# Small empty products ahead of the first scores of a fused attention and two-stage expert kernel

## The chip, the cores and the metric

The kernel runs on one core of a Trainium2 chip. The metric is the time of one execution on the device in microseconds; of three runs of the kernel before, the median is 618.53 us (618.53 to 618.88). A profiled execution gives the trace: what each engine did and when, counted from the first instruction.

## The reference

```python
# attention: 2 batches, 8 heads, 576 positions, head size 64
scores = scale * np.matmul(q, k.transpose(0, 1, 3, 2))
# heads 0-3: the last 32 positions; heads 4-7: every 32nd position before
mask_local = (rel >= 0) & (rel < stride)
mask_strided = (rel >= 0) & (pos[None, :] % stride == pos[:, None] % stride)
attn = softmax(where(mask, scores, -1e9)); x = attn @ v          # -> (1152, 512)
# gated block
h = (x @ w1) * (x @ w2) @ w3;  x = h @ w_out
# four experts, weighted by the normalised domain probabilities
out += p[:, e:e + 1] * (np.maximum(x @ w1[e], 0.0) @ w2[e])
```

All inputs and outputs are float32; the weights of the gated block are 64-bit floats that the kernel turns into pairs of 32-bit parts itself.

## The kernel before, in words

The order of the instructions on every engine is written out by hand, in the order of the Python statements; a wait is inserted wherever one engine needs another's result. Each engine works through its own list in order.

The attention of a batch is cut into six chunks (`Chunk4`): chunks 0 to 2 are local heads, 3 to 5 strided ones. For a chunk, `scores` (L380) puts a mask product (L386 or L395) and then many small products of 64 rows (L391, L402) into one PSUM bank; `maxima`, `subtract`, `exps` and `sums` turn them into weights on VectorE and ScalarE, `normalise` (L450) runs on GpSimd for the first batch; `transposes` (L455), `evac` (L460), `pv` (local values L475, strided values L484) and `put` (L513) follow. The chunks are interleaved by hand: scores of chunks 0, 1, 2, 3, then the transposes of chunk 0, scores of 4, transposes of 1, scores of 5, values of 0 and so on.

Queries and keys of the first local heads are loaded in two halves, cut at position 288 (`load_qk(0, 0, CUT)`): chunk 0 needs the first half, chunk 1 the second. Value loads and the first weight load follow on SyncE's queue; the weight load waits behind a one-element write on GpSimd (`hold`, L128), which stands in GpSimd's list behind the normalisation of chunk 2.

An empty product multiplies a zeroed tile `idle` by itself into a bank that nobody reads. `warm_up` issues two of 512 columns right after the tile is zeroed, ahead of the first scores (`keep_warm(WARM)`, L120); `keep_warm` puts in three more between the chunks' scores and the transposes, one of 512 and two of 256 columns. A product of float32 operands is recorded as two matmuls, each with a weight load of its own.

After the attention of the first batch, the products of x with the first two weights (`whole_product`, L616), the gated block (`ab_block`, L305 to L307), the third weight, and the experts follow, on TensorE nearly without a gap.

Of the kernel before, what the change touches and what calls it, by code (L numbers as in the profile page):

```python
# [19 lines left out]
W = 32  # L20
# [10 lines left out]
NBLK = NT // BLK  # L31
NTT = NT // P
NEG = -8.0e9
WARM = 2
SCALE = 1.0 / float(D) ** 0.5

EXP_LO, EXP_HI = 3.0517578125e-05, 122880.0
# [7 lines left out]
def kernel(  # L45
# [14 lines left out]
    mm = nc.tensor.matmul  # L60
# [13 lines left out]
    def bank(name):  # L74
        return ps.tile([P, 512], F32, tag="ps", name=name)
# [33 lines left out]
    def warm_up():  # L109

        idle = tmp.tile([P, P], F32, tag="pT", name="idle")
        nc.vector.memset(idle, 0.0)
        nc.scalar.activation(small.tile([P, 1], F32, tag="rec", name="one"), idle[:, :1], AF.Exp)
        moving = idle.unsqueeze(1).to_broadcast([P, 4, P])

        def keep_warm(n, parts=4):
            if n:
                acc = bank("idle").rearrange("p (a b) -> p a b", a=4)[:, :parts]
            for i in range(n):
                mm(acc, idle, moving[:, :parts], start=i == 0, stop=i == n - 1)  # L120

        keep_warm(WARM)
        return keep_warm


# [725 lines left out]

    with tc.manual_schedule():
        keep_warm = warm_up()
        load_qk(0, 0, CUT)
        local_masks()
# [166 lines left out]
        for n in range(2):  # L1022
            acc = bank("ab_acc")[:, :HB]
# [37 lines left out]
        for it in range(8):  # L1061
# [8 lines left out]
            i = {1: 0, 3: 1, 6: 2}.get(it)  # L1070
# [139 lines left out]
```

## Time and profile before

| | |
|---|---|
| median of 3 runs | 618.53 us (618.53 to 618.88) |
| profiled execution | 618.26 us, of which the span of its instructions 616.1 us |
| TensorE matmuls | busy 609.8 us (99%), 4488 recorded |
| VectorE | busy 443.1 us (72%) |
| ScalarE | busy 280.6 us (46%) |
| GpSimd | busy 9.9 us (2%) |
| share of the chain that ended last | TensorE 90%, VectorE 4%, ScalarE 3%, DMA 2%, issue 1% |

The chain is followed back from the last instruction, at each step to what released it. "issue" is time in which an engine waited for nothing that the profile shows. Overlapping matmuls are drawn with their full length each, so a group's time in the timeline runs a little past the start of the next group.

### The profile page before, as it was taken

The page shows a single profiled execution, that of the slowest core. Times are in us where ns is not written, and L with a number is a line of the kernel's source. Part 1 is how long each engine was busy: PE and PEld are TensorE (multiplying, and loading weights), DVE is VectorE, ACT ScalarE, POOL GpSimd, SP SyncE. Part 2 cuts the span into 40 slices and gives each one's busy share as a digit, 9 for nine tenths or more (in the row PEclk, how much of TensorE's full clock was granted, in tenths as well). Part 3 has the DMA queues.
Part 4 walks back from the last instruction along what each step waited for, and adds up shares of the span by engine and source line. Part 5 has one row for each costly group of instructions (what it writes and reads, how often), then busy time and mean ns, then how long its engine had stood idle before and what let it go on. Part 6 is the DMA issues. An engine that isn't in the chain of part 4 may idle for free.

```text
span 616.1 us, 11131 instructions
## 1 busy us (share of the span) xinstructions
PE 609.8 (99%) x4488; PEld 555.9 (90%) x4488; DVE 443.1 (72%) x811; ACT 280.6 (46%) x568; POOL 9.9 (2%) x33
## 2 busy tenths in 40 slices
PE   8999999999999999999999999999999999999997
PEld 5799999998889999998899988999889898989997
DVE  4899987998863237777877987887766665755843
ACT  3879966665733134333433333434343333333320
POOL 4100000000000000000000000000000000000000
PEclk9999999999999999999999999999999999999999
DMA  9896330334522202333545334435585557464411
GB/s 272 321 325 185 139 138 2 111 132 172 202 68 102 86 19 69 137 138 136 199 153 194 128 149 172 167 142 212 178 318 202 213 192 248 162 234 176 156 51 68
DMA packets 28510, 99.63 MB, mean 162 GB/s; under 512 B 2660, under 2 KB 6316, under 8 KB 26028
## 3 DMA queue, kind: packets, MB, share of 16 engines
q1 hardware_dynamic: 27916, 98.34, 44.5%
q8 instruction: 35, 0.57, 0.4%
q10 hardware_dynamic: 544, 0.59, 0.3%
q14 instruction: 15, 0.12, 0.1%
HBM read 79.78 MB, written 19.14 MB: 161 GB/s over the span
## 4 chain that ended last, share of the span: by engine, by line
PE 90%; DVE 4%; ACT 3%; DMA 2%; issue 1%; DVEq 0%; ACTq 0%; SPq 0%
PE g_acc L305 11%; PE g_acc L306 11%; PE g_acc L307 11%; PE m_a L307 4%; PE m_a L306 4%; PE m_a L305 4%; PE ab_acc L305 3%; PE ab_acc L307 3%; PE ab_acc L306 3%; PE m_b L306 3%; PE m_c L305 3%; PE m_c L306 3%; PE m_b L305 3%; PE x_acc L305 3%; PE m_c L307 3%; PE m_b L307 3%
## 5 line engine op out<-in xcount | busy, mean ns | idle before, releaser
L761 ACT ACTIVATE h_hi<-u 128x320 fp32r<-128x320 f32 (+1 forms) x128 | 56.9, 445 | 188.9 <-DVE u L767 188.9
L305 PE MATMUL g_acc<-w_hi,h_hi 128*128 128x512 f32 (+1 forms) x296 | 114.3, 386 | 0.0
L306 PE MATMUL g_acc<-w_lo,h_hi 128*128 128x512 f32 (+1 forms) x296 | 114.2, 386 | 0.0
L307 PE MATMUL g_acc<-w_hi,h_lo 128*128 128x512 f32 (+1 forms) x296 | 113.7, 384 | 0.0
L700 DVE TENSOR_TENSOR w_lo<-raw,w_hi 128x768 fp32r<-128x768 f32 x64 | 69.3, 1084 | 12.3 <-ACT w_hi L698 12.3
L767 DVE TENSOR_TENSOR u<-m_b,u 128x320 f32<-128x320 f32 (+1 forms) x96 | 40.7, 451 | 50.4 <-PE m_b L307 50.4
L305 PE MATMUL ab_acc<-x_hi,w_hi 128*128 128x288 f32 x240 | 71.6, 298 | 0.4 <-ACT ab L601 0.2
L307 PE MATMUL ab_acc<-x_hi,w_lo 128*128 128x288 f32 x240 | 70.7, 295 | 0.0
L306 PE MATMUL ab_acc<-x_lo,w_hi 128*128 128x288 f32 x240 | 70.7, 294 | 0.0
L307 PEld LDWEIGHTS g_acc<-w_hi,h_lo 128*128 128x128 f32 x296 | 55.6, 188 | 11.6
L305 PEld LDWEIGHTS g_acc<-w_hi,h_hi 128*128 128x128 f32 x296 | 55.8, 188 | 8.0
L306 PEld LDWEIGHTS g_acc<-w_lo,h_hi 128*128 128x128 f32 x296 | 55.7, 188 | 7.6
L763 DVE SCALAR_TENSOR_TENSOR h_lo<-u,h_hi 128x320 fp32r<-128x320 f32 (+1 forms) x128 | 57.6, 450 | 3.6 <-ACT h_hi L761 1.1
L698 ACT CAST w_hi<-raw 128x768 fp32r<-128x768 f32 x64 | 59.9, 936 | 0.0
L305 PEld LDWEIGHTS ab_acc<-x_hi,w_hi 128*128 128x128 f32 x240 | 45.0, 188 | 1.0 <-ACT ab L601 0.5
L306 PEld LDWEIGHTS ab_acc<-x_lo,w_hi 128*128 128x128 f32 x240 | 45.0, 188 | 0.0
L307 PEld LDWEIGHTS ab_acc<-x_hi,w_lo 128*128 128x128 f32 x240 | 45.0, 188 | 0.0
L306 PE MATMUL m_b<-b_t,s_hi 128*128 128x320 f32 (+1 forms) x128 | 37.9, 296 | 0.0
L767 DVE TENSOR_TENSOR u<-m_a,u 128x320 f32<-128x320 f32 (+1 forms) x64 | 28.8, 449 | 11.6 <-PE m_a L307 11.6
L700 DVE TENSOR_TENSOR s_lo<-raw,s_hi 128x1024 fp32r<-128x1024 f32 x16 | 19.6, 1225 | 24.3 <-ACT s_hi L698 24.3
L767 DVE TENSOR_TENSOR u<-m_c,u 128x320 f32<-128x320 f32 (+1 forms) x64 | 28.9, 452 | 4.5 <-PE m_c L307 3.9
L777 ACT COPY u<-m_a 128x320 f32<-128x320 f32 (+1 forms) x32 | 12.7, 398 | 42.4 <-PE m_a L307 42.4
(180 smaller groups left out, 1384.6 us busy)
## 6 DMA issues: line engine op xcount, KB each, us to landing
raw<-in_e_dram SPq DMA_DIRECT2D x32, 1024.0 KB, 4.9
raw<-in_w3T_dram SPq DMA_DIRECT2D x8, 1024.0 KB, 4.9
stored<-s_hi SPq DMA_DIRECT2D x16, 512.0 KB, 2.6
stored<-s_lo SPq DMA_DIRECT2D x16, 512.0 KB, 2.6
s_hi<-stored SPq DMA_DIRECT2D x16, 512.0 KB, 3.7
s_lo<-stored SPq DMA_DIRECT2D x16, 512.0 KB, 4.9
raw<-in_w_dram SPq DMA_DIRECT2D x7, 1024.0 KB, 7.2
raw<-in_w_out_dram SPq DMA_DIRECT2D x4, 1024.0 KB, 5.0
```

Source lines behind the costliest of these rows:

```text
L305: mm(acc, lh, rh, start=first, stop=False)
L306: mm(acc, lh, rl, start=False, stop=False)
L307: mm(acc, ll, rh, start=False, stop=last)
L698: nc.scalar.copy(dst[0], src)
L700: nc.vector.tensor_tensor(out=dst[1], in0=src, in1=dst[0].bitcast(F32), op=ALU.subtract)
L761: nc.scalar.activation(hi, src, AF.Relu)
L763: nc.vector.scalar_tensor_tensor(out=lo, in0=src, scalar=0.0, in1=hi.bitcast(F32), op0=ALU.max, op1=ALU.subtract)
L767: nc.vector.tensor_tensor(out=out, in0=acc, in1=b, op=ALU.add)
L777: nc.scalar.copy(u1, a)
```

## The change

The two empty products of 512 columns ahead of the first scores become 18 of 32 columns, in turn on the lower and the upper 64 rows and columns of the array, and one of 256 columns. The later empty products stay.

```diff
-WARM = 2
+FILL = 18
...
-        keep_warm(WARM)
+        acc = bank("idle")
+        for i in range(FILL):
+            r = slice(64 * (i % 2), 64 * (i % 2) + 64)
+            mm(acc[r, :W], idle[r, :64], idle[r, :W], start=True, stop=True)
+        keep_warm(1, 2)
         return keep_warm
```

`W` is 32; `keep_warm(1, 2)` is one product of 2 x 128 columns. The lines of the kernel move down by four.

TensorE's list begins like this before, up to the scores of chunk 1 (`sc` is a chunk's scores, `tqk` the queries and keys, `i_loc` and `m_loc` the local mask):

```order
L1206 UNCONDITIONAL_BRANCH
L120 MATMUL idle<-idle 128x512 x2
L386 LDWEIGHTS i_loc
L386 MATMUL sc<-m_loc,i_loc 128x384
L391 MATMUL sc<-tqk 32x64 x24
L386 LDWEIGHTS i_loc
L386 MATMUL sc<-m_loc,i_loc 128x384
L391 MATMUL sc<-tqk 32x64 x24
```

And like this after the change, the same stretch:

```order
L1210 UNCONDITIONAL_BRANCH
L125 MATMUL idle<-idle 64x32 x18
L120 MATMUL idle<-idle 128x256
L390 LDWEIGHTS i_loc
L390 MATMUL sc<-m_loc,i_loc 128x384
L395 MATMUL sc<-tqk 32x64 x24
L390 LDWEIGHTS i_loc
L390 MATMUL sc<-m_loc,i_loc 128x384
L395 MATMUL sc<-tqk 32x64 x24
```

Nineteen products stand where two stood; what follows is the same. Further down, TensorE's list after the change has the scores of chunk 3, the transposes of chunk 0 (`tp`) and the scores of chunk 4 (`i_str` and `m_str` are the strided mask):

```order
L399 LDWEIGHTS i_str
L399 MATMUL sc<-m_str,i_str 128x432
L406 MATMUL sc<-tqk 54x54 x16
L459 MATMUL tp<-ident,p_ring 128x128 x3
L399 LDWEIGHTS i_str
L399 MATMUL sc<-m_str,i_str 128x432
L406 MATMUL sc<-tqk 54x54 x16
L459 MATMUL tp<-ident,p_ring 128x128 x3
```

These rows are those of before, with 17 more products ahead of them. The lists of the other engines are unchanged.

## Rows read from the trace of the kernel before

**Rows 1.** The page: span, busy time of the matmul engine, instruction queue (packets, MB).
```profile
span 616.1 us, 11131 instructions
...
PE 609.8 (99%) x4488; PEld 555.9 (90%) x4488; DVE 443.1 (72%) x811; ACT 280.6 (46%) x568; POOL 9.9 (2%) x33
...
q8 instruction: 35, 0.57, 0.4%
```
**Rows 2.** Groups of matmuls, 0 to 10.7 us (xcount | busy us, mean ns | idle before).
```profile
L120 PE MATMUL idle<-idle 128*128 128x512 f32 (+1 forms) x8 | 5.6, 819 | 1.0 <-DVE idle L112 1.0
L391 PE MATMUL sc<-tqk 64*32 64x64 f32 x144 | 3.3, 249 | 0.1
L386 PE MATMUL sc<-m_loc,i_loc 128*128 128x384 bf16 x3 | 1.3, 431 | 0.0
```
**Rows 3.** Timeline of the matmuls (start us, us, instruction, xcount, idle before).
```profile
1.05 3.78 PE L120 MATMUL idle<-idle 128*128 128x512 f32 x4 [1.05 <-DVE idle L112]
...
5.08 1.51 PE L391 MATMUL sc<-tqk 64*32 64x64 f32 x48
...
7.09 0.87 PE L391 MATMUL sc<-tqk 64*32 64x64 f32 x48
...
10.46 0.35 PE L395 MATMUL sc<-m_str,i_str 128*128 128x432 bf16 x1
10.73 1.01 PE L402 MATMUL sc<-tqk 64*54 64x54 f32 x32
11.67 0.55 PE L455 MATMUL tp<-ident,p_ring 128*128 128x128 f32 x3
12.05 0.35 PE L395 MATMUL sc<-m_str,i_str 128*128 128x432 bf16 x1
12.33 0.95 PE L402 MATMUL sc<-tqk 64*54 64x54 f32 x29
14.18 0.30 PE L402 MATMUL sc<-tqk 64*54 64x54 f32 x3 [0.90 <-issue]
```
**Rows 4.** Groups of matmuls between the two stops, 14.1 to 18.1 us.
```profile
L475 PE MATMUL o<-pT,tv_loc 64*64 64x32 f32 x85 | 1.7, 220 | 0.0
L402 PE MATMUL sc<-tqk 64*54 64x54 f32 (+1 forms) x35 | 1.2, 198 | 0.9 <-issue 0.9
L455 PE MATMUL tp<-ident,p_ring 128*128 128x128 f32 x6 | 1.1, 291 | 0.0
L395 PE MATMUL sc<-m_str,i_str 128*128 128x432 bf16 x1 | 0.3, 346 | 0.0
```
**Rows 5.** The chain of waits up to 24 us (start us, us, what).
```profile
1.54 5.41 DMA tqk<-in_qT_dram
...
10.80 0.94 PE sc L402 x32
...
17.84 0.30 issue
...
20.66 0.60 PE tp L455 x4
...
23.03 0.81 PE o L484 x32
```
**Rows 6.** Instruction packets in 11.36:12.74, 15.3:16.75, 19.4:20.45 us (share of 16 engines).
```profile
q8 instruction: 1, 0.02, 6.2%
...
q8 instruction: 1, 0.02, 5.6%
...
q8 instruction: 1, 0.02, 5.5%
```
**Rows 7.** Timeline of VectorE: the maxima of chunks 3 and 4.
```profile
11.79 0.61 DVE L408 TENSOR_REDUCE mx<-sc 128x8 f32<-128x432 f32 x1 [0.21 <-PE sc L402]
...
14.52 0.61 DVE L408 TENSOR_REDUCE mx<-sc 128x8 f32<-128x432 f32 x1 [0.60 <-PE sc L402]
```
**Rows 8.** Busy time of each engine from 23.9 to 600 us.
```profile
23.90:600.00 576.10, 575.52 (x3895) 529.75 (x3896) 422.09 (x766) 266.43 (x527) 0.00 (x0) 1.00 0.44 160
```

## The prediction

> **What bounds the kernel now.** I read the page first, then the matmul engine's timeline, the chain of waits, and last the instruction packets among the DMA traffic. The page says that TensorE is busy for 609.8 of 616.1 us [rows 1]. From 23.9 us to 600 us it idles for 0.6 us in all [rows 8]. So whatever shifts the start of that dense stretch shifts the end by the same amount, and a change in the first 23 us is worth what it does to the chain there: the strided value products that start at 23.03 us [rows 5], behind which the dense work queues.
>
> Before that, three things hold TensorE up. Until 6.96 us the chain is the load of the second half of the queries [rows 5]; the second chunk's scores start at 7.09 us [rows 3] and nothing ahead of them in the program can bring that forward. Then TensorE runs without a gap to 13.28 us, stops for 0.90 us inside the fifth chunk's scores, 29 of 32 records done [rows 3], and stops again for 0.30 us at 17.84 us [rows 5]. Both stops have the releaser "issue": no engine and no load that the profile shows is waited for.
>
> What those two stops have in common is an instruction count. The trace records 4488 matmuls and 4488 weight loads, and the instruction queue q8 fetched 35 packets of 0.57 MB / 35 = 16 KB [rows 1]; 8976 / 35 = 256 records to a packet. Between the two stops lie 85 + 35 + 6 + 1 = 127 matmuls [rows 4], with their loads 254 records, plus a few waits. So TensorE stops where one packet of 256 instructions ends and the next is not there yet. The packets fit: the first starts at 11.36 us and takes 0.062 x 16 x 1.38 = 1.37 us, and TensorE goes on 1.45 us after its end, at 14.18 us. The next takes 0.056 x 16 x 1.45 = 1.30 us from 15.39 us; its end at 16.69 us and the restart at 18.14 us are again 1.45 us apart. The third takes 0.055 x 16 x 1.05 = 0.92 us, from 19.47 us [rows 6]; by the same 1.45 us it is usable at 21.84 us.
>
> [...]
>
> **The change part by part.** Two products of 512 columns are four matmul records; 18 small ones and one of 256 columns are, at two records a product, 38. The matmuls' waits and everything behind them stay as they are.
>
> *The time of the products themselves.* The old four fill 1.05 to about 4.6 us, 0.89 us each. The 256-column product is two records of half that, 0.9 us. Eighteen small ones have no row. The nearest is the strided chunk's scores, which also alternate two 64-row corners: 32 records in 0.94 us at the full clock [rows 5], so 59 ns each at half the clock, 36 x 59 ns = 2.1 us. Lower bound, by the first scores (48 in 1.51 us [rows 3]): 36 x 31 ns = 1.1 us. Upper bound, by a quarter of a 128-column transpose (0.55 / 3 [rows 3]) at half the clock: 3.3 us. I take 2.1, by the nearest row: the first mask product then starts at 4.1 us instead of 4.6, within 3.1 to 5.3. Both ends are worth nothing at the end of the kernel. Earlier first scores wait for 6.96 us all the same; later ones push the second chunk by at most 0.5 us, which the longer stop below swallows.
>
> *The place of the packets' borders.* Thirty-four more matmuls with their loads put 68 instructions in front. Each border therefore moves 34 matmuls earlier. The first stop stood ahead of the 222nd matmul: 8 + 144 + 3 records [rows 2] and the strided mask's 1, then 32, 3, 1 and 29 [rows 3]. It now stands ahead of what was the 188th, the very last record of the fourth chunk's scores. Before, that record was done at 11.74 us.
>
> *When the packet comes.* It is asked for, I take it, when the sequencer passes the border one packet earlier: 127 matmuls before the 222nd, so at the 95th, formerly. That ran at about 7.65 us inside the second chunk's scores, and was handed over between 7.0 us, when their load came, and then. The border moves to the 61st, still behind the wait for 6.96 us, so to 7.0 us at best. The packet thus comes 0 to 0.65 us earlier; I take 0.2, since an engine that is given instructions ahead of running them passes a border early. TensorE restarts at 13.98 us, within 13.53 and 14.18.
>
> *The sum.* At 13.98 us TensorE still has what lies between 11.74 and 13.28 us in the old trace, 1.54 us, and one record, 0.03. It reaches the old stop's place at 15.55 instead of 14.18 us: 1.37 us late. The stop of 0.30 us goes, since the next packet, 3.96 us after the restart as before (18.14 less 14.18), is there at 17.94 us and its border is reached at 17.1 + 1.37 = 18.5 us. That leaves 1.07 us. The packet after it is usable 3.70 us later (21.84 less 18.14), at 21.64 us. Its border, 34 matmuls earlier, falls near the end of the first strided values, which ended at 20.66 us [rows 5] and now would at 21.73: just in time, where it had half a microsecond to spare. The other way round this packet could take as long as the first, which came 3.7 us after its border ran instead of 1.3; then it costs 2.4 us. The first weight load's hold stands on GpSimd behind a normalisation that depends on the delayed scores, so its megabyte moves into this packet's way; I add 0.2 us, with 0 and 2.4 kept for the range. VectorE's path gives much the same: the maxima at 11.79 us wait until 14.2, the next ones come at 14.2 + (14.52 - 0.60 - 11.79) = 16.3 instead of 14.52 us [rows 7], 1.8 us late, of which the slack ahead of the later transposes takes up most, so it hides behind TensorE's 1.07.
>
> So +1.27 us on the profiled 618.26 us is 619.5; the median of the timed runs is 618.53, 0.27 above it: **619.8 us**. About 0.2%, 1.24 us, is what a measurement of this kernel can tell from no change, so this forecast lies on that line, a little beyond it.
>
> **The rivals.**
> *Asked for before the wait (not slower).* The new border is only a dozen instructions behind the 6.96 us wait. If the sequencer asks that far ahead of what it hands over, the packet is asked for with the first scores, at about 4.7 us; the 4.1 us from 7.2 to 11.36 us, 1.37 and 1.45 us later it is there at 11.6 us, and the stop of 0.90 us is gone. Then the 0.30 us can go too, and the packet after costs about 0.5 us again, since all comes 1.2 us sooner: 618.53 - 0.7 = 617.8 us. It decides at a lead of about 13 instructions. Against it: the first packet came 3.7 us after its border ran, so nothing was asked for very early.
> *The late packet.* The 2.4 us above come in most part: 618.53 + 1.07 + 2 = 621.6 us. For it: the DMA engines are loaded; against: the packets asked for at 14.18 and 18.14 us came within 1.3 us.
> *No tie to the count.* The stops come from the queue's load at that time and not from the border; the profile only infers "issue". Then nothing on the chain changes: 618.5 us. Against it stand the 127.
> [...]
> [...]
>
> **How the numbers follow.** Forecast 0.45 (0.27 beyond the 0.2% line, 0.18 inside it); asked before the wait 0.15 (0.08 faster, 0.07 the same); late packet 0.12; no tie 0.20 (0.17 the same, 0.02 faster, 0.01 slower); clock 0.08. That is faster 0.10, same 0.42, slower 0.48. The forecast's own range, restart 13.53 to 14.18 us and a little more or less of the last wait, is 619.3 to 620.2; the range for 8 in 10 reaches to most of the first and second rival: 617.7 to 621.6 us.
>
> **What would show it.** In the new trace the first "issue" stop should stand at the end of the fourth chunk's scores, one record short, from about 11.7 to 14.0 us, with the maxima behind it; there should be none inside the second local values; the strided values ahead of the dense stretch should start near 24.3 instead of 23.03 us. A stop at the old place, or none, breaks the forecast at the border; a first packet that starts well before 11.1 us breaks it at the time of asking; second-chunk scores that take 1.5 us speak for the clock.

## The result and the profile after

The changed kernel takes 624.06 us (median of 5 runs, 623.76 to 624.6) against 618.53 us (5 runs, 618.2 to 618.88): 1.0092 times as long, 95% interval 1.0077 to 1.0106. The forecast was 619.8 us, its range 617.7 to 621.6; the time lies above the range. The profiled execution took 623.93 us, 5.67 us more than that of before.

The page after, to set beside [rows 1]:

```profile
span 621.8 us, 11199 instructions
...
PE 611.5 (98%) x4522; PEld 558.6 (90%) x4522; DVE 443.3 (71%) x811; ACT 280.3 (45%) x568; POOL 9.8 (2%) x33
...
q8 instruction: 35, 0.57, 0.4%
```

TensorE has its 34 more records and 1.7 us more of busy time; the span grew by 5.7 us, so some 4 us of that are idle time. The timeline of the matmuls after, for [rows 3] and the end of [rows 5]:

```profile
1.05 2.14 PE L125 MATMUL idle<-idle 64*64 64x32 f32 x36 [1.05 <-DVE idle L112]
3.11 1.22 PE L120 MATMUL idle<-idle 128*128 128x256 f32 x2
4.13 0.53 PE L390 MATMUL sc<-m_loc,i_loc 128*128 128x384 bf16 x1
...
7.07 1.32 PE L395 MATMUL sc<-tqk 64*32 64x64 f32 x48 [0.30 <-DMA tqk<-in_qT_dram]
...
11.15 1.00 PE L406 MATMUL sc<-tqk 64*54 64x54 f32 x31
13.90 0.20 PE L406 MATMUL sc<-tqk 64*54 64x54 f32 x1 [1.75 <-issue]
...
14.69 1.61 PE L406 MATMUL sc<-tqk 64*54 64x54 f32 x32
...
21.93 0.68 PE L488 MATMUL o<-pT,tv_str 54*64 54x54 f32 x28
23.89 0.32 PE L488 MATMUL o<-pT,tv_str 54*64 54x54 f32 x4 [1.28 <-issue]
...
26.57 0.81 PE L488 MATMUL o<-pT,tv_str 54*64 54x54 f32 x32 [0.28 <-ACT pT L464]
```

The reader is to see two stops with the releaser "issue", ending at 13.90 and 23.89 us, and that the strided values ahead of the dense stretch start at 26.57 instead of 23.03 us [rows 5]: 3.54 us late. The next chunk's 32 records behind the first stop took 1.61 us, where the same form took 1.01 before [rows 3]. Why, the windows tell (stretch, its length, busy time of PE, PEld, DVE, ACT and POOL, granted clock, DMA share, GB/s):

```profile
14.00:16.00 2.00, 2.00 (x36) 1.69 (x36) 1.79 (x4) 1.04 (x2) 0.00 (x0) 0.72 0.85 172
16.00:18.00 2.00, 2.00 (x32) 1.30 (x30) 1.80 (x5) 0.79 (x2) 0.91 (x3) 0.50 0.02 9
...
23.90:600.00 576.10, 573.46 (x3931) 527.10 (x3931) 422.10 (x764) 268.14 (x532) 0.00 (x0) 1.00 0.44 162
```

After the stop the granted clock was 0.50 of full speed from 14.88 to 18.30 us. And the long stretch from 23.9 us idles for 576.10 - 573.46 = 2.64 us, where [rows 8] had 0.58: some 2 us more went far behind the change. The waits of TensorE (us in all, times, longest) show one there:

```profile
PE sc L406 <- issue: 1.7, 1, 1.7
PE ab_acc L309 <- ACT ab L605: 1.7, 1, 1.7
PE o L488 <- issue: 1.3, 1, 1.3
```

The second row is the gated block's, at 143 us. With each matmul of after put beside the same one of before (by their order in the traces), the delay is 3.54 us when the dense stretch starts, grows by 0.55 us at 133.26 us (129.18 before) and by 1.56 us at 143.15 us (137.51 before), and stays: 3.54 + 0.55 + 1.56 = 5.65 of the 5.67 us. Three places are to be explained.

**The start, 3.54 us.** The chain behind the first stop, in the timelines of VectorE, GpSimd and SyncE:

```profile
14.14 0.61 DVE L412 TENSOR_REDUCE mx<-sc 128x8 f32<-128x432 f32 x1 [2.14 <-PE sc L406]
...
16.42 0.83 POOL L454 TENSOR_TENSOR p_ring<-p_ring,rec 128x384 f32<-128x384 f32 x1 [3.40 <-DVE rec L450]
17.19 0.10 POOL L132 MEMSET raw<- 128x1 int32 x1
...
17.32 0.84 SPq L164 DMA_DIRECT2D raw<-in_w_dram  x2
```

The same two places of before:

```profile
14.07 0.83 POOL L450 TENSOR_TENSOR p_ring<-p_ring,rec 128x384 f32<-128x384 f32 x1 [1.47 <-DVE rec L446]
...
14.96 0.84 SPq L160 DMA_DIRECT2D raw<-in_w_dram  x2
```

The maxima of chunk 3 are 2.35 us late (11.79 in [rows 7]). Behind them in VectorE's list stand the sums that chunk 2's normalisation needs, so the normalisation on GpSimd is 2.35 us late too, and with it the hold behind it and the two halves of the first weight load, a megabyte (2.36 us). The third instruction packet starts at 21.67 us, 2.20 us after that of before, and 4.35 us after the halves' issue (4.51 before). The packet in the DMA traffic of after, 21.6 to 22.65 us:

```profile
q8 instruction: 1, 0.02, 5.6%
```

It took 0.056 x 16 x 1.05 = 0.94 us; 1.28 us after its end TensorE goes on, at 23.89 us (1.45 us at both stops of before).

**The 0.55 and 1.56 us.** The chain of waits after holds two loads of the third weight (start, us):

```profile
117.42 6.26 DMA raw<-in_w3T_dram
...
134.41 5.50 DMA raw<-in_w3T_dram
```

Before, the same loads took 4.79 and 4.73 us; the second of them in its chain:

```profile
129.46 4.73 DMA raw<-in_w3T_dram
```

In the traffic of after from 117.45 to 118.65 us, a packet starts within the first load:

```profile
q8 instruction: 1, 0.02, 5.5%
issues: line engine op xcount, KB each, median us to landing
raw<-in_w3T_dram SPq DMA_DIRECT2D x1, 1024.0 KB, 6.3
```

It starts at 117.52 us, 0.10 us after the issue. Fifteen of the load's sixteen pieces had landed 4.61 us after the issue, the last after 6.26. The second load's packet starts 0.75 us after its issue. Before, the packets of this stretch came at 118.80 us, just after the first load had landed (113.90 + 4.79), and at 135.65, 1.5 us after the second had (129.46 + 4.73). So the packets moved 4.8 and 5.4 us forward against the issues of the two loads. Together the loads took 1.47 + 0.77 = 2.24 us longer than before, which is the 2.11 us of delay to within 0.13.

### The profile page after: what moved, and what is told of

Same layout as the page of the kernel before. It is cut to its first block, busy times and chain, and to the rows that moved or that the text cites. A ratio compares the mean times of both kernels' runs of the same rounds, so it can differ in the third digit from the quotient of the medians.

```text
span 621.8 us, 11199 instructions
## 1 busy us (share of the span) xinstructions
PE 611.5 (98%) x4522; PEld 558.6 (90%) x4522; DVE 443.3 (71%) x811; ACT 280.3 (45%) x568; POOL 9.8 (2%) x33
## 4 chain that ended last, share of the span: by engine, by line
PE 86%; DVE 6%; ACT 3%; DMA 3%; issue 2%; DVEq 0%; SPq 0%; ACTq 0%
PE g_acc L309 11%; PE g_acc L310 11%; PE g_acc L311 11%; PE m_a L311 4%; PE m_a L310 4%; PE m_a L309 4%; PE m_b L310 3%; PE m_c L309 3%; PE m_c L310 3%; PE m_b L309 3%; PE x_acc L309 3%; PE m_c L311 3%; PE m_b L311 3%; PE x_acc L310 3%; PE x_acc L311 3%; PE wc_acc L309 2%
```

## The experiments

Times are medians of the timed runs, with the kernel before on the same chip in the same hour. In the sets of several rounds the kernel before itself ran from 617.8 to 622.0 us; differences of some tenths are read from the profiles, not from medians. A diff that has `FILL` is against the changed kernel, and so are those of load_first and after_late12; that of values_later is against early26, the others against the kernel before. `...` stands for lines left out.

**few** has lighter work ahead without the count: one product of 512 and one of 256 columns.

```diff
-        keep_warm(WARM)
+        keep_warm(1)
+        keep_warm(1, 2)
```

> One empty product of 512 columns and one of 256 ahead of the first scores: a quarter less of the old products, but only two more matmul records than before instead of 34. If the number of instructions is what costs (they move the packet borders), the first stop stands 2 records earlier than before, 27 of the fifth chunk's 32 records done, about 0.9 us long, and the time is that of before, 618.5 us within 0.5. If it is the shorter or lighter work ahead of the scores that costs (a clock that rises late or falls), the time is above 620 us and the second chunk's 48 records take 1.3 us or more and the stop is where it was.

618.8 us, 1.0007 (0.9992 to 1.0022). The expectation counts two records too many: two products stand where two stood, and 4488 matmuls are recorded as before. Its matmuls:

```profile
14.13 0.30 PE L403 MATMUL sc<-tqk 64*54 64x54 f32 x3 [0.85 <-issue]
...
18.36 0.42 PE L476 MATMUL o<-pT,tv_loc 64*64 64x32 f32 x11 [0.57 <-issue]
```

The old stops stand at the old places (0.90 and 0.30 us before). A quarter less work ahead of the first scores costs nothing that ten runs could tell; by the profile the dense stretch starts 0.21 us late.

**ten** has 10 small products and the one of 256 columns: 18 records more than before, where the change has 34.

```diff
-FILL = 18
+FILL = 10
```

> 10 small products instead of 18, then the 256-column one: 18 records more than before. Packet theory: the first stop stands ahead of what was the 204th matmul, 11 of the fifth chunk's 32 records done, at about 12.7 us, and lasts to about 14.0 us, so 1.3 us, and is shorter than the 1.75 us of the changed kernel; whether the clock falls behind it is open. Early loss about 0.7 us without the clock, up to 2.5 with it; later borders come 2.3 us earlier and one packet falls into a weight load near 115 to 119 us, 0 to 2 us more: 619.2 to 621.5 us. If small products as such cost, the loss is about 10/18 of the changed kernel's 5.5 us: 621.6 us.

619.35 us, 1.0012 (1.0001 to 1.0023).

```profile
14.40 0.71 PE L406 MATMUL sc<-tqk 64*54 64x54 f32 x21 [0.85 <-issue]
...
18.90 0.66 PE L479 MATMUL o<-pT,tv_loc 64*64 64x32 f32 x29 [0.67 <-issue]
```

The stops stand ahead of the old 204th and 331st matmul: each 18 records earlier than the 222nd and 349th, as the count asks. The granted clock stays at 1.00 (14 to 18 us and 23.9 to 600 us), and the start of the dense stretch is 1.0 us late (24.02). No packet starts within 4 us behind the issues of the third weight's two loads; they take 4.87 and 5.15 us, and the delay grows by 0.46 us there. The place of the stops follows the count. The first stop lasts 0.85 us, as in few, and not the 1.75 us of the changed kernel: it starts at 13.55 instead of 12.15 us. Small products as such, at 10/18 of the loss, would have made 621.6 us.

**early26** moves the first border ahead of the wait at 6.96 us, so that its packet is asked for earlier: 26 small products, none of 256 columns.

```diff
-FILL = 18
+FILL = 26
...
-        keep_warm(1, 2)
```

> 26 small products and none of 256 columns: the same length ahead of the scores, 48 records more than before. The border at which the first packet is asked for now lies in the first chunk's scores, ahead of the wait for the second half of the queries. If a packet is asked for when the border is passed, it starts 2 us or more before 11.1 us, and the first stop, now inside the fourth chunk's scores with 17 of 32 records done, shrinks to 0.5 us or less, the clock stays up: 617.5 to 619.5 us. If the load queue alone decides when it comes, it comes at 11.1 us as before, the stop lasts from 11.2 to 13.9 us, the clock falls again: 624 us or more.

623.74 us, 1.0085 (1.0059 to 1.011), where 617.5 to 619.5 us were expected.

```profile
12.55 0.60 PE L405 MATMUL sc<-tqk 64*54 64x54 f32 x15 [0.56 <-issue]
...
18.21 0.32 PE L478 MATMUL o<-pT,tv_loc 64*64 64x32 f32 x7 [1.35 <-issue]
```

The first packet did come earlier, at 9.85 us, and the first stop shrank to 0.56 us. The second did not follow (15.38 us, as at 15.39 before), so a second stop of 1.35 us arose, and the granted clock was 0.50 from 18.80 to 25.62 us. Here the earlier packet only moved the wait to the next.

**late17** leaves the early part alone and adds 17 small products after the second batch's first three score chunks (their tile `zeros` is filled early).

```diff
+        late_products(17)
```

> The kernel before with 17 small empty products behind the second batch's first three score chunks, at about 35 us: the same 34 records more, but behind the first stops, so nothing changes before 35 us. The products themselves cost 34 x 30 ns = 1.0 us. Theory for the loss behind 110 us: the instruction packets now start 3 to 4 us earlier against the loads, fall into the two loads of the third weight that the chain waits for, one piece of 16 of each comes late, and TensorE waits up to 2 us more near 130 to 137 us: 620.5 to 621.7 us. If that loss has another cause (the delay of the early part itself), it stays at 619.5 us.

622.99 us (619.21 to 625.81), 1.0059 (1.0032 to 1.0085), above the 620.5 to 621.7 us expected. The early stops were much as before (0.56 and 0.57 us). A stop came that was not planned, here in the matmul timeline:

```profile
37.82 0.30 PE L115 MATMUL late<-zeros 64*64 64x32 f32 x3 [1.98 <-issue]
```

Behind it the windows show the granted clock at half:

```profile
38.00:40.00 2.00, 2.00 (x11) 1.96 (x10) 1.26 (x2) 0.00 (x0) 0.00 (x0) 0.51 1.08 438
```

And the late loss is there, 1.36 us of waiting ahead of 143.04 us, with both loads of the third weight in the chain:

```profile
117.97 5.90 DMA raw<-in_w3T_dram
...
134.62 5.14 DMA raw<-in_w3T_dram
```

Packets had started 0.08 and 0.81 us after their issues. So the late loss needs no early stop. But of this profile's 5.5 us some 4.1 stood already at 100 us, from the added products, the stop and the clock, and the late loss made 1.46 us; by this run alone the early delay could be its cause as well as the packets.

**busy** asks whether the stop or the clock behind it is what costs: 16 small products, and two more of 512 columns ahead of chunk 3's scores, which fill the stop and leave the borders behind them where the change has them.

```diff
-FILL = 18
+FILL = 16
...
+        keep_warm(2)
```

> The changed kernel with 16 small products instead of 18 and two more empty products of 512 columns ahead of the fourth chunk's scores: as many instructions ahead of the border as in the changed kernel, but TensorE works some 1.8 us longer before it stops, so that the stop is nearly gone while the packet comes when it came. Theory: the restart stays at 13.9 us within 0.3, the stop is 0.5 us or less, the clock does not fall behind it, the fifth chunk's 32 records take 0.95 us instead of 1.61, and 1.7 us come back: 622.3 us. Rival, the stop's length itself is what costs, by whatever way: the restart comes later by the added work and the time is 624 us or more. Rival, the fall of the clock has nothing to do with the stop: the fifth chunk still takes 1.6 us, 624 us.

626.24 us, 1.0125 (1.0095 to 1.0155), where 622.3 us were expected. Its matmuls:

```profile
12.92 1.08 PE L406 MATMUL sc<-tqk 64*54 64x54 f32 x32
...
14.59 1.01 PE L406 MATMUL sc<-tqk 64*54 64x54 f32 x32
...
23.93 0.32 PE L488 MATMUL o<-pT,tv_str 54*64 54x54 f32 x4 [2.38 <-issue]
```

No first stop, and 1.01 instead of 1.61 us for chunk 4: where the stop was gone, the clock did not fall (1.00 from 14 to 24 us). Yet the second stop ends at 23.93 us, where it ended at 23.89. Its first weight's halves tell why (SyncE's timeline):

```profile
17.22 0.84 SPq L164 DMA_DIRECT2D raw<-in_w_dram  x2
```

The added products end chunk 3's scores at the same time as the stop did, so the halves are issued at nearly the same time (17.32 in after) and the packet starts at 21.56 us (21.67). The border that asks for it was passed at 18.21 us instead of 19.73: 1.5 us earlier, and worth nothing. After this longer stop, of 2.38 us, the granted clock was 0.50 from 25.24 to 32.07 us, and the delay grew from 3.83 us at the start of the dense stretch to 6.24 us at 40 us. The second load of the third weight took long here too:

```profile
135.49 6.15 DMA raw<-in_w3T_dram
```

Hence a time above the change's.

**load_first** is the change with the hold of the first weight load moved ahead of chunk 2's normalisation in GpSimd's list, so that the megabyte passes before the third packet. `scale_of(2)` holds that normalisation.

```diff
-        exp_of(3)
-        scale_of(2)
         zero.whole_load()
         loaded = 1
+        exp_of(3)
+        scale_of(2)
```

> The changed kernel with the first weight load (a megabyte) moved ahead of the third chunk's normalisation in GpSimd's order, so that it no longer waits for the delayed scores. Theory: the packet that caused the second stop, 1.28 us at the end of the first strided values, was behind this load; it starts at 20.5 us or earlier instead of 21.67, the second stop shrinks below 0.5 us: 622.8 to 623.3 us, unless the load now delays the packet at 15.5 us instead, in which case a stop appears inside the second local values and the time stays at 624. Rival, the load has nothing to do with it: the stop stays at 1.3 us, 624.0 us.

625.92 us, 1.0111 (1.0066 to 1.0156), but from 621.52 to 627.84 in 4 runs, where 622.8 to 623.3 us were expected; **load_first_2**, the same kernel beside **after_2**, the changed kernel again:

> The kernel with the earlier weight load again. Its profile had no second stop and its first time was 621.5 us, but two others were 627.7. Theory: the profile shows no second stop again and the strided values ahead of the dense stretch start near 24.6 us instead of 26.6; the times fall into two groups, about 621.5 to 622 where the clock stays up and 3 us or more above that where it falls; the lowest is below the lowest of the changed kernel. Rival: the 621.5 was a stray one, and all times are at 624 or above.

> The changed kernel again, on the chip and in the hour of the two below, since single times of the last kernels spread by 4 to 6 us. Theory: its second stop ends when the third packet is in, at 23.9 us within 0.2, whatever the clock did before, and one piece of the first load of the third weight comes late; 623.5 to 625 us, with little spread unless the clock falls behind the second stop.

623.75 us (6 runs, 620.62 to 624.12) for load_first_2 and 624.38 us (4 runs, 623.27 to 627.61) for after_2: by the medians the time gained is not told from nothing. The profiles tell the mechanism; those of load_first and load_first_2 are of their fastest runs, 621.52 and 620.62 us. SyncE and the matmuls of load_first:

```profile
14.35 0.84 SPq L164 DMA_DIRECT2D raw<-in_w_dram  x2
...
14.04 0.20 PE L406 MATMUL sc<-tqk 64*54 64x54 f32 x1 [0.59 <-issue]
...
21.11 1.13 PE L488 MATMUL o<-pT,tv_str 54*64 54x54 f32 x32
...
24.62 0.81 PE L488 MATMUL o<-pT,tv_str 54*64 54x54 f32 x32 [0.31 <-ACT pT L464]
```

With the halves at 14.35 us the packet starts at 19.17, the second stop is gone (all 32 values at once), and the dense stretch is 1.59 us late instead of 3.54 (1.27 in load_first_2; 3.74 in after_2). Not all of that is the load's: in these two profiles the first stop was 0.59 and 0.85 us, shorter than the 1.75 us of after, and no fall of the clock followed it (1.00 from 14 to 18 us in both). The late loss stayed, since the borders did; the chain of load_first:

```profile
115.51 6.20 DMA raw<-in_w3T_dram
```

**after_late12** is the change with 12 small products late, as in late17, which move the later packets away from the loads.

```diff
+        late_products(12)
```

> The changed kernel with 12 small empty products behind the second batch's first score chunks: 24 records, 0.7 us of TensorE at the full clock. They move the later packets some 3 us earlier against the loads, to about 115 and 132 us, ahead of the two loads of the third weight (issued near 118 and 134 us) instead of just behind their issue. Theory: both loads land in about 4.8 us with no piece late, the 2.1 us between 130 and 143 us come back and 0.7 us are paid: 622.7 us. Rival, the loss there follows from the early delay and not from the packets: 624.8 us.

624.79 us, 1.0096 (1.0065 to 1.0127). The chain:

```profile
118.92 5.04 DMA raw<-in_w3T_dram
...
134.71 4.94 DMA raw<-in_w3T_dram
```

With packets at 115.91 and 133.27 us, ahead of both issues, the loads land as before, and the delay grew by 0.4 us between 110 and 143 us instead of 2.1. The total did not fall, because the profiled run lost more early: the granted clock was 0.50 twice, from 13.73 to 17.15 and from 23.97 to 27.39 us, and the dense stretch started 4.89 us late. The loads' part is borne out, the total is not; that it comes to the rival's 624.8 us is chance, since the late loss that the rival kept is gone.

**sum** puts busy, load_first and the 12 late products together.

> All three edits together on the changed kernel (16 small products and two of 512 columns before the border, the first weight load earlier, 12 small products late). If the four causes are all there are (longer first stop, fall of the clock, second stop, late weight loads), what is left is the later restart, about 0.9 us, and the 0.7 us of the late products: 620.1 us within 0.7. If something else is in the 5.5 us, it stays above 621.5 us.

621.59 us (621.38 to 624.76), 1.0063 (1.0038 to 1.0087), 0.8 over the upper end of what was expected and just above the 621.5 us from which on something else was to be in the loss. Its matmuls:

```profile
24.81 0.81 PE L496 MATMUL o<-pT,tv_str 54*64 54x54 f32 x32 [0.30 <-ACT pT L472]
...
37.52 0.30 PE L403 MATMUL sc<-tqk 64*32 64x64 f32 x3 [0.85 <-issue]
```

Neither early stop is left, the loads land in 4.83 and 4.79 us, and 2.4 of the 5.5 us are gone, though the kernel does more work. What remains is a dense stretch that starts 1.78 us late, a stop of 0.85 us at another border, which the expectation had not counted, and the late products (0.8 us).

**values_later** is early26 with the strided value loads held on GpSimd until chunk 1's normalisation, to see whether the second packet waits behind these loads.

```diff
-    def load_v_str(b):
+    def load_v_str(b, held=False):
...
+        hold(held, tv[:, 0, :1])
...
-        load_v_str(0)
-        load_v_rest(0)
...
+        load_v_str(0, True)
+        load_v_rest(0)
```

> 26 small products and none of 256 columns, and the strided value loads (640 KB) held back until the second chunk is normalised, so that they are not in the way of the second packet. Theory: the first stop is 0.6 us or less, as with 26 products before; the second packet, asked for at 12.5 us, starts near 14 us instead of 15.4, the second stop (1.35 us before) shrinks below 0.4 us, the clock stays up: 617.5 to 619 us, so the kernel before is met or beaten by up to 1 us. Rival: the second packet comes at 15.4 us all the same, the stop stays: 623 us or more.

621.75 us, 1.0033 (1.0015 to 1.0052), where 617.5 to 619 us were expected, and 2 us better than early26. The second packet came at 13.25 us instead of 15.38, and both stops of early26 are gone; but

```profile
22.54 0.79 PE L488 MATMUL o<-pT,tv_str 54*64 54x54 f32 x18 [2.35 <-issue]
```

the third packet started at 20.30 us, behind the weight halves (issued at 16.02 us), though its border had been passed at 16.24, and the granted clock was 0.50 from 22.23 to 25.64 us.

**none** has no product at all ahead of the first scores.

```diff
-WARM = 2
+WARM = 0
```

> The kernel before without any empty product ahead of the first scores: 4 records less. Theory: the first stop stands behind the fifth chunk's scores, among the second transposes, at about 14.2 us for its end, the second near the end of the second local values at 18.1 us; if the clock rises only with the scores, the lost time ends in the stop, which shrinks: 618.3 us within 0.7. Rival, the empty products ahead of the scores are needed for the clock: it rises after 10 us and the time is 620 us or more.

619.56 us, 1.0006 (0.9993 to 1.0018): no change by the medians. The full clock (1.00) is on record only from 10.79 us, where before has it from 6.76 us; the second chunk's 48 records took 1.50 us instead of 0.87, chunk 3's scores started at 12.49 instead of 10.73 us [rows 3], and the halves and the third packet were late here too (16.72 and 21.79 us), with a stop ahead of the last values:

```profile
23.98 0.93 PE L484 MATMUL o<-pT,tv_str 54*64 54x54 f32 x41 [0.88 <-issue]
```

The products of x start 1.1 us later than in before (24.84 against 23.76 us). So most of what the products ahead win by the clock lies under the waits for the queries and the packets, and no more than about 1 us is left, which ten runs don't tell from nothing.

The third packet over the profiles. The border that asks for it is taken to be passed where the 349th matmul starts, the place of the second stop of before:

| kernel | halves issued | border passed | packet starts |
|---|---|---|---|
| before | 14.96 | 18.14 | 19.47 |
| few | 14.96 | 18.36 | 19.79 |
| ten | 15.69 | 18.90 | 20.65 |
| values_later | 16.02 | 16.24 | 20.30 |
| early26 | 16.37 | 16.64 | 20.70 |
| none | 16.72 | 18.29 | 21.79 |
| busy | 17.22 | 18.21 | 21.56 |
| after | 17.32 | 19.73 | 21.67 |
| after_2 | 17.23 | 19.63 | 21.63 |
| after_late12 | 17.23 | 19.63 | 21.67 |
| late17 | 14.93 | 18.04 | 19.36 |
| load_first | 14.35 | 18.45 | 19.17 |
| load_first_2 | 14.01 | 18.38 | 19.13 |
| sum | 13.88 | 18.92 | 19.62 |

In the first eleven the packet starts 4.3 to 5.1 us after the halves' issue, whatever the border did (1.3 to 4.1 us); in the last three, where the halves were early, 0.70 to 0.75 us after the border and 4.8 to 5.7 us after the halves. The two kernels to compare are busy and load_first: they passed the border at nearly the same time, 18.21 and 18.45 us, and the packet starts at 21.56 and 19.17 us, the halves having been issued at 17.22 and 14.35. So the packet waits behind the megabyte. That reading of the table was made after the runs. What in the megabyte the packet waits for, they don't settle: in thirteen of the fourteen the packet starts 0.2 to 0.9 us after the first half has landed, but in values_later 3 us before.

The two loads of the third weight can be read over all profiles too. In each of the thirteen besides before, TensorE's delay grows between 120 and 150 us by what the two loads took beyond the 4.79 and 4.73 us of before, to within 0.1 us: from 0.10 us in sum to 2.1 us in the changed kernel. It does not follow the delay that was there: after_late12 came with 5.0 us and lost 0.38, early26 with 3.9 and lost 0.18, load_first with 1.6 and lost 1.87. So the late loss is the loads' length, and not the early delay.

## Why the prediction was wrong, step by step

- *What bounds the kernel; the packets.* Right for the start. 256 instructions to a packet (8976 records in 35 packets) placed the first stop exactly: 31 of 32 records of chunk 3's scores done, restart at 13.90 us (13.98 predicted), none inside the second local values, the next border 28 records into the first strided values ("near the end"). few, with the old count, and ten tie it to the count; the rival without a tie to the count falls. The stops of 1.75 and 1.28 us stand at the borders.
- *The small products.* Right: 2.14 us for 36 records (2.1), first mask product at 4.13 us (4.1). The half clock in that estimate was an assumption: before and after have no record of the clock so early (the first, of 1.00, begins at 6.76 and 8.06 us); what the profile of after shows is the 256-column product, whose start and that of the next group lie 1.02 us apart at 3.11 us and 0.53 us at 10.34 us. few agrees that lighter work there is worth nothing at the end, though it has no small products.
- *When the first packet comes.* Right: 11.08 us, 0.28 earlier than in before (0.2 taken; that the engine is given its instructions ahead of running them was an assumption). That a packet is asked for at the border one packet earlier was the author's assumption too: no run shows how many packets TensorE holds, and in before the second and third started 1.21 and 1.33 us after the restarts at the two borders. It was not asked for before the wait; in early26, where the border lay ahead of the wait, it was, and the time was lost again at the next one.
- *The sum, third packet.* This is the step that failed. The prediction named the cause, the hold behind the normalisation that moves the megabyte into the packet's way, and gave it 0.2 us with 2.4 as the bound. The rows had the working for more: the maxima were taken to be 2.4 us late, and they stand ahead of that normalisation in VectorE's order. Carried on, 19.47 + 2.4 gives a start at 21.9 us. It was 21.67, where the prediction's arithmetic gives 21.64 less 1.45 and some 0.9, thus 19.3. The border was passed late as well, at 19.73 instead of 18.5 us, but busy passed it at 18.21 and won nothing. The rest of the sum gave 1.07 us, so with 3.54 us at the start of the dense stretch the term measured 2.47 us instead of 0.2. The second rival, the late packet (0.12), has the size; its reason, a packet that takes 3.7 us from its border, is not what was seen (1.94 us, behind a megabyte that came late), so the 2.4 us fit in part by luck.
- *VectorE's path hides behind TensorE's 1.07 us.* Wrong for the same reason: its delay came back through GpSimd and the DMA queue as TensorE's second stop.
- *The clock.* The chance of 0.08 came true in part: a granted clock of 0.50 from 14.88 to 18.30 us, behind the first stop of 1.75 us. In busy it stayed at 1.00 where the stop was gone. What this cost, 0.6 us in chunk 4 and more behind it, lay under the wait for the third packet. At the start, where the prediction looked for it, the second chunk's 48 records took 1.32 us instead of 0.87, which the first stop covered. In the traces the record of the full clock (1.00) begins at 8.06 us in after and at 6.76 us in before. Over all profiles it begins at 3.9 to 6.8 us in the three with large products ahead (before, few, late17), at 6.9 to 11.0 us in the ten with small ones and at 10.8 us in none: behind small products it began later, with a wide spread, and the waits for the queries and the packets lay over it.
- *"Whatever shifts the start shifts the end by the same amount."* Wrong by 2.1 us of 5.65. This is the second step that failed, a term put at nothing because the stretch idles for 0.6 us before; with 2.47 us for the one and 2.1 for the other the sum comes to 618.53 + 1.07 + 2.47 + 2.1 = 624.2 us. The sum knew two kinds of instruction packets, those that TensorE waits for and those that it doesn't; it had not asked what the latter collide with. late17 (loss without an early stop), after_late12 (early stop without the loss) and the lengths of the loads over all profiles show that the loads' length makes the loss. That a packet close behind the issue makes a load long is what the profiles mostly show: of the two loads of each profile, ten had a packet within 0.9 us behind the issue; nine of these landed in 5.1 to 6.3 us and one, in early26, in 5.00, while 4.7 to 5.2 us was usual without. Two without took longer: 5.39 us in load_first_2, its packet 0.16 us ahead of the issue, and 6.15 us in busy, its packet 4.0 us behind it, where ten had one 4.3 us behind and 5.15 us. Which piece is hit, and when it matters, the runs don't settle.

## What to carry to other kernels

Count instructions, not work, when something small is put ahead of a long program: every packet's border moves (here by 34 matmuls), and a stop, a load's delay or a slower clock may turn up far from the edit, as the loss at 133 and 143 us did here. When a stop shifts one engine, follow its delay through the other engines' lists to the transfers that they release, and ask what waits behind those in the DMA queues. A price that can be worked out from rows along such a chain is worked out, not allowed for.

## What had not been expected of the hardware

An instruction packet of 16 KB (0.57 MB in 35), 0.9 to 1.4 us by itself, started 4.3 to 5.1 us after a megabyte that had been issued ahead of it in eleven profiles, and 0.70 to 0.75 us after its border in the three where that load had been issued 4.1 to 5.0 us ahead of the border. The other way round, with a packet close behind a load's issue one piece of sixteen landed 1.65 us behind the other fifteen (6.26 against 4.61 us). In few another load of the third weight, issued at 136.07 us with a packet 0.01 us behind, shows the same, 6.89 against 5.00 us, and TensorE's delay hardly grew there (0.10 us). And stops of 1.35 to 2.4 us in an engine that is otherwise busy were followed by 3.4 to 6.8 us at a granted clock of 0.50 in six kernels, but not always: the changed kernel kept 1.00 after its second stop of 1.28 us, and in after_2 after one of 1.58 us, where it had fallen after the first of 1.56 us.
